# A planned attention and SoLU kernel: loads laid out by partition, and other rules for whom an engine waits

## Chip, cores and metric

One core of one Trainium2 chip runs the whole program. The metric is device time in microseconds, the median of three runs; one more execution is taken by the profiler.

## What is computed

The reference is attention with a local window of 16 positions and block summaries, followed by a two-layer block with a SoLU and a normalisation between its products:

```python
batch, n_heads, seq, head_dim = (4, 8, 768, 64)
block, window = (32, 16)
k_sum = k.reshape(B, H, nb, block, D).max(axis=3)
v_sum = v.reshape(B, H, nb, block, D).mean(axis=3)
scores_l = scale * np.matmul(q, k.transpose(0, 1, 3, 2))
mask_l = np.abs(pos[:, None] - pos[None, :]) < window
scores_s = scale * np.einsum('bhsd,bhnd->bhsn', q, k_sum) + np.log(block)
a = softmax(np.concatenate([np.where(mask_l, scores_l, -1e9), scores_s], axis=-1))
x = np.matmul(a, np.concatenate([v, v_sum], axis=2))    # then (3072, 512)
h = x @ w_in                                            # (3072, 1024)
solu = h * softmax(h)
ln = (solu - mean) / np.sqrt(var + 1e-06) * g_ln
return ln @ w_out                                       # (3072, 512)
```

## The kernel before

The 3072 tokens are 24 tiles of 128 (t). Two tiles make a group of 256 positions (4 windows of 64 positions), three groups (g) a batch (b). Names end in b_g_pp where they belong to an attention unit, which is one group and one half (pp) of the heads: unit 1_0 is group 1, half 0 of a batch. Per unit TensorE forms the scores `s` of 64 positions against a window of 96 keys and 24 block maxima (L498), VectorE takes maxima while adding the mask (L518), ScalarE the exponentials (L526) and their sum z (L531), VectorE its reciprocal (L532), POOL or VectorE the product `e` times 1/z (L245, L246), TensorE transposes (`t`, L552) and multiplies by the values `vt` (`x`, L590). `x` is split into a high and a low part (`xh`, `xl`), and so are the weights, so that each product with w_in (`h`, L616) and w_out (`o`, L681) is three matmuls.

There is one PSUM buffer `h`. Tile t+1 may write it only when VectorE has read tile t twice: the maximum `hm` (L623) and, after ScalarE's exponential `he` (L625), its sum `hz` (L627) and the reciprocal (L628), the product L629. The rest (mean, squares on ScalarE, L636 to L652), the transposes `lt` and `o` follow, `o` three tiles behind.

The weights come as 64-bit numbers in 8 pieces of w_in and 8 of w_out, 512 KB each (`raw`), and are rounded and split by some seven operations a piece (L315 to L334, then L356 to L358 or L238 to L246) on ScalarE, VectorE and POOL, between the attention of the first tiles.

Loads are issued on SyncE's queue. Keys (`kraw`, 400 KB each) are 128 x 800 numbers; queries (`qt`) are 512 KB in pieces of 1 KB, in the first group four loads of 128 KB; the rows of the first batch's values (`st_v`, L388) are three loads of 512 KB in pieces of 2 KB; the windows of values (`vt`, L457) are 768 KB, 96 partitions with four overlapping windows each, in pieces of 2 KB. Into rows 96 to 119 of `vt` ScalarE's queue copies the block means `vsum` (L462), marked as another part of the buffer, so that it need not wait for L457. `LOADS` (L44) is the order of the first loads.

The order on every engine is worked out when the program is built. `Plan.issue` takes each operation with a cost, its data dependences and a due number (the place in the program of the TensorE operation that needs it first), and always starts what can start first; `WAIT` and `FAR` say for whom an engine waits instead, and `RATE` gives a load's duration. Each engine then runs its list strictly in that order, so one operation that waits holds all behind it. Until `FILL` the plan puts short matmuls on zeros (L766, "fillers") where it sees TensorE idle. The rule about waiting is:

```python
            for at, y in ready[e]:
                s = begin(e, at)
                if t < s and s - t < self.WAIT * (t + cost(e, o, t) - s) and y.due + self.FAR < best[1].due:
                    best = (s, y)
```

Of the kernel before, what the change touches and what calls it, by code (L numbers as in the profile page):

```python
# [68 lines left out]
class Plan:  # L69
# [8 lines left out]
    WAIT, FAR = 1.5, 200  # L80
# [49 lines left out]
    def issue(self):  # L130
# [47 lines left out]
        while len(order) < len(self.ops):  # L178
# [32 lines left out]


@with_exitstack
def attn_then_solu(ctx: ExitStack, tc: tile.TileContext, q, k, v, vb, w_in, w_out, g_ln, out):


    nc = tc.nc
    plan = Plan()
    op = plan.op
    pe, act, dve, pool, sp = "pe", "act", "dve", "pool", "sp"  # L220
# [42 lines left out]
    for p0 in (0, QT):  # L263
# [7 lines left out]
            out=m, in_=m, pattern=[[0, 3], [-1, WIN]], compare_op=ALU.is_ge, fill=NEG,  # L271
# [111 lines left out]

    def load_v_rows(b, i):

        rows = v[b, HALO + 2 * P * i:HALO + 2 * P * (i + 1), :].rearrange("(c p) n -> p c n", p=P)
        vst[b, i] = x = plan.buf(sb, [P, 2, 512], F32, "lh" if i < 2 else "ll", 2, f"st_v{b}_{i}")
        op(sp, 0.05, lambda: nc.sync.dma_start(out=x.ap, in_=rows), w=[x], nbytes=P * 4096)  # L388

    def mean_values_first(b):  # L390

# [47 lines left out]
           r=[acc], w=[y])  # L439

    def load_q(b, g, pairs=None, after=()):
        src = q[b, :, :, g * G * QT:(g + 1) * G * QT].rearrange("a p c -> p a c")
        if (b, g) not in qt:
            qt[b, g] = plan.buf(sb, [P, NPAIR, G * QT], F32, "qt", 2, f"qt{b}_{g}")
        x = qt[b, g]
        if pairs is None:
            op(sp, 0.05, lambda: nc.sync.dma_start(out=x.ap, in_=src), w=[x], nbytes=P * 4096,
               after=after)
        else:
# [221 lines left out]
    def second(t):  # L671
# [130 lines left out]
```

## Time and profile before

| | us |
|---|---|
| median of 3 runs | 419.6 (417.32 to 420.45) |
| profiled execution | 419.72 |
| its span, first to last instruction | 417.9 |
| TensorE busy | 396.2 (95%) |
| VectorE busy | 284.1 (68%) |
| ScalarE busy | 243.6 (58%) |
| POOL busy | 124.2 (30%) |
| waits of TensorE's `h` for VectorE's L629 | 6.9 in 7 waits |

PE is TensorE's matmuls and PEld its weight loads, DVE is VectorE, ACT ScalarE, POOL GpSimd, SP SyncE. A busy share is an average over stages with different limits: an engine that is idle elsewhere may be full in the stage that matters. In a timeline row the bracket gives the idle time of the engine just before, and what ended it. The granted clock (PEclk) is a fraction of 2.4 GHz.

### The profile page before, as it was taken

To read this page: it belongs to the slowest core of one execution; us is meant where nothing else is said; L and a number is where in the kernel's file an instruction comes from. 1 tells how busy PE (TensorE), PEld (TensorE's weight loads), DVE (VectorE), ACT (ScalarE), POOL (GpSimd) and SP (SyncE) were. 2 spreads that over 40 slices of the span, in tenths; PEclk is the share of its full clock that TensorE was granted. 3 is DMA by queue.
4 is the path that set the end of the run, shared out by engine and by line. 5 is a ranking of instruction groups with operands and counts; after the bars stand their busy time and mean duration, and the time that the engine had idled before them with its cause. 6 is when DMAs were issued, how large, how long until landed. Compare 5 with 4: busy or idle time off the path is not lost.

```text
span 417.9 us, 9489 instructions
## 1 busy us (share of the span) xinstructions
PE 396.2 (95%) x3667; PEld 299.3 (72%) x3667; DVE 284.1 (68%) x841; ACT 243.6 (58%) x710; POOL 124.2 (30%) x172
## 2 busy tenths in 40 slices
PE   7999598889899999999999999999999999999996
PEld 3437376567678777777877777777777777777876
DVE  4998899996877776736876764564676567453440
ACT  4967889737556745745763673675675566332231
POOL 4676546887851101108102110110110100111010
PEclk9999879999999999999999999999999999999999
DMA  8999996428337412126134220241230000000011
GB/s 268 410 256 263 327 245 164 127 78 197 91 117 200 130 49 80 52 88 153 55 100 124 77 78 27 76 102 40 77 95 29 25 6 23 27 25 2 25 50 52
DMA packets 22929, 46.03 MB, mean 110 GB/s; under 512 B 1860, under 2 KB 8260, under 8 KB 22884
## 3 DMA queue, kind: packets, MB, share of 16 engines
q1 hardware_dynamic: 18096, 36.97, 31.4%
q10 hardware_dynamic: 4788, 8.46, 6.2%
q8 instruction: 29, 0.48, 0.5%
q14 instruction: 16, 0.13, 0.1%
HBM read 36.97 MB, written 6.29 MB: 104 GB/s over the span
## 4 chain that ended last, share of the span: by engine, by line
PE 58%; DMA 16%; DVE 15%; ACT 5%; POOL 3%; issue 1%; SPq 0%; DVEq 0%
PE h L616 26%; PE o L681 22%; DMA kraw<-in_k 4%; DMA vt<-in_v 4%; DMA raw<-in_w_out 4%; DVE hm L623 3%; DVE e L518 3%; DVE he L629 3%; ACT he L625 3%; PE x L590 3%; PE lt L552 3%; DMA st_v<-in_vb 2%; PE t L552 2%; PE s L498 2%; POOL st_v L418 2%; DMA raw<-in_w_in 2%
## 5 line engine op out<-in xcount | busy, mean ns | idle before, releaser
L616 PE MATMUL h<-w,xh 128*128 128x512 f32 x384 | 141.1, 405 | 8.2 <-DVE he L629 6.9
L681 PE MATMUL o<-w,lh 128*128 128x512 f32 (+1 forms) x400 | 142.4, 394 | 0.1
L616 PEld LDWEIGHTS h<-w,xh 128*128 128x128 f32 x384 | 72.4, 189 | 31.8 <-issue 11.0
L681 PEld LDWEIGHTS o<-w,lh 128*128 128x128 f32 x400 | 74.1, 188 | 19.0 <-issue 2.9
L681 PE MATMUL o<-w,ll 128*128 128x512 f32 (+1 forms) x200 | 77.2, 386 | 0.5 <-DVE ll L666 0.5
L616 PE MATMUL h<-w,xl 128*128 128x512 f32 x192 | 75.7, 394 | 0.0
L526 ACT ACTIVATE e<-e,nm 128x120 f32<-128x120 f32 x192 | 73.0, 384 | 1.1 <-DVE nm L518 1.1
L636 POOL TENSOR_SCALAR he<-he,nmu 128x512 f32<-128x512 f32 x27 | 23.8, 883 | 99.5 <-DVE nmu L632 99.3
L625 ACT ACTIVATE he<-h,hm 128x1024 f32<-128x1024 f32 x24 | 26.7, 1114 | 42.9 <-DVE hm L623 42.8
L238 ACT COPY at<-t 120x512 f32<-120x512 f32 x45 | 24.2, 587 | 41.5 <-PE t L552 41.4
L681 PEld LDWEIGHTS o<-w,ll 128*128 128x128 f32 x200 | 37.6, 188 | 8.0 <-DVE ll L666 0.8
L518 DVE CUSTOM_DVE_ANT_0 e<-s,mask 128x120 f32<-128x120 f32 x192 | 40.5, 275 | 2.8 <-PE s L498 2.8
L616 PEld LDWEIGHTS h<-w,xl 128*128 128x128 f32 x192 | 36.3, 189 | 6.8
L623 DVE TENSOR_REDUCE hm<-h 128x1 f32<-128x1024 f32 x24 | 29.3, 1221 | 14.9 <-PE h L616 14.9
L240 POOL COPY kw<-ksum 128x192 f32<-128x192 f32 (+1 forms) x26 | 9.4, 363 | 100.6 <-PE s L498 79.9
L641 ACT ACTIVATE sq<-he 128x1024 bf16<-128x1024 f32 x24 | 25.4, 1057 | 22.6 <-POOL he L636 20.6
L239 DVE CAST lh<-lt 128x512 fp32r<-128x512 f32 x23 | 15.8, 687 | 32.4 <-PE lt L552 27.1
L666 DVE TENSOR_TENSOR ll<-lt,lh 128x512 fp32r<-128x512 f32 x48 | 31.8, 684 | 8.5 <-ACT lh L238 8.1
L418 POOL TENSOR_TENSOR st_v<-st_v 96x512 f32<-96x512 f32 (+3 forms) x42 | 33.9, 816 | 8.8 <-DMA st_v<-in_vb 6.3
L526 ACT ACTIVATION_READ_ACCUMULATOR e<-e,nm 128x1 f32 x192 | 36.3, 189 | 0.0
L590 PEld LDWEIGHTS x<-at,vt 120*64 120x64 f32 (+1 forms) x768 | 25.4, 141 | 10.4 <-issue 5.2
L629 DVE SCALAR_TENSOR_TENSOR he<-h,hz,he 128x1024 f32<-128x1024 f32 x24 | 30.7, 1278 | 0.2
(79 smaller groups left out, 525.3 us busy)
## 6 DMA issues: line engine op xcount, KB each, us to landing
vt<-in_v SPq DMA_DIRECT2D x12, 768.0 KB, 5.8
kraw<-in_k SPq DMA_DIRECT2D x16, 400.0 KB, 7.5
out<-os ACTq DMA_DIRECT2D x23, 256.0 KB, 2.0
qt<-in_q SPq DMA_DIRECT2D x11, 512.0 KB, 4.0
st_v<-in_vb SPq DMA_DIRECT2D x12, 384.0 KB, 3.7
raw<-in_w_in SPq DMA_DIRECT2D x8, 512.0 KB, 7.1
raw<-in_w_out SPq DMA_DIRECT2D x8, 512.0 KB, 12.0
vt<-vsum ACTq DMA_DIRECT2D x11, 192.0 KB
```

What stands on the lines that cost most here:

```text
L238: by = {act: lambda: nc.scalar.copy(out=to(), in_=of()), dve: lambda: nc.vector.tensor_copy(out=to(), in_=of()), pool: lambda: nc.gpsimd.t ...
L418: op(pool, 0.15 + w * 0.0021, lambda w=w, o=o: nc.gpsimd.tensor_tensor(out=o.ap[:n, :w], in0=x.ap[:n, :w], in1=x.ap[:n, w:2 * w], op=ALU.add),
L518: nc.vector.tensor_tensor_reduce(out=e.ap[:, n, :], in0=sc.ap[:, j, (2 * i + up) * KC:(2 * i + up + 1) * KC], in1=mask[:, mi, :], scale=-S ...
L526: nc.scalar.activation(out=e.ap[:, n, :], in_=e.ap[:, n, :], func=AF.Exp, bias=nm.ap[:, n:n + 1], scale=-1.0, accum_out=z.ap[:, n:n + 1])
L590: nc.tensor.matmul(xp.ap[j * D:(j + 1) * D, i, qs], vs.ap[:k, u, cs], at.ap[:k, u % 2, n[j] + u // 2, :], start=not apart, stop=not apart ...
L616: nc.tensor.matmul(o, a.ap[:, c, ts], w.ap[:, i], start=(c == 0 and n == 0), stop=(c == NKC - 1 and n == 2))
L623: op(dve, 1.13, lambda: nc.vector.tensor_reduce(out=nm.ap, in_=h.ap, op=ALU.max, axis=AX.X, negate=True), r=[h], w=[nm])
L625: op(act, 1.09, lambda: nc.scalar.activation(out=e.ap, in_=h.ap, func=AF.Exp, bias=nm.ap, accum_out=z.ap), r=[h, nm], w=[e, z])
L629: op(dve, 1.27, lambda: nc.vector.scalar_tensor_tensor(out=e.ap, in0=h.ap, scalar=z.ap, in1=e.ap, op0=ALU.mult, op1=ALU.mult, accum_out=s1 ...
L641: op(act, 1.13, lambda: nc.scalar.activation(out=sq.ap, in_=e.ap, func=AF.Square, accum_out=ss.ap), r=[e], w=[sq, ss])
L666: op(dve, 0.6, lambda part=part, r=r: nc.vector.tensor_tensor(out=part(lo), in0=tp.ap[:, r], in1=part(hi).bitcast(F32), op=ALU.subtract), ...
L681: nc.tensor.matmul(o.ap[:, cols], a.ap[:, f, :], w.ap[:, i, cols], start=(f == 0 and n == 0), stop=(f == NFC - 1 and n == 2))
```

## The change

Arrays are laid out on the host so that what a partition gets in one load lies in one piece of memory: keys by pairs, queries by group (4 KB a partition; the first group in two loads of 256 KB instead of four), the value rows (4 KB) in an array of their own, and the windows of values over 128 partitions (8 KB each, 1 MB; rows 96 to 127 are zeros). The window load now writes the whole buffer, so the copy of the block means comes after it. In the plan, `RATE` goes from 360 to 400, `WAIT` from 1.5 to 4.0 and `FAR` from 200 to 40: an engine waits for what is due 40 places earlier, not 200, and up to four times as long as the wait saves.

```diff
-LOADS = "kqkqkqkqwwwwwwwwrrrvQV"
+LOADS = "kqkkqkwwwwwwwwrrrvQV"
...
-    RATE = 360.0
+    RATE = 400.0
...
-    WAIT, FAR = 1.5, 200
+    WAIT, FAR = 4.0, 40
...
-        op(sp, 0.05, lambda: nc.sync.dma_start(out=x.ap[:, i], in_=k[b, p]), w=[(x, i)], nbytes=P * SP * 4,
+        op(sp, 0.05, lambda: nc.sync.dma_start(out=x.ap[:, i], in_=k[b, pp, :, i]), w=[(x, i)], nbytes=P * SP * 4,
...
-        rows = v[b, HALO + 2 * P * i:HALO + 2 * P * (i + 1), :].rearrange("(c p) n -> p c n", p=P)
-        op(sp, 0.05, lambda: nc.sync.dma_start(out=x.ap, in_=rows), w=[x], nbytes=P * 4096)
+        op(sp, 0.05, lambda: nc.sync.dma_start(out=x.ap, in_=vr[i]), w=[x], nbytes=P * 4096)
...
-            op(sp, 0.05, lambda: nc.sync.dma_start(out=x.ap[:, pairs], in_=src[:, pairs]),
-               w=[(x, pairs)], nbytes=P * 1024)
+        part = slice(None) if pairs is None else slice(2 * pairs, 2 * pairs + 2)
+        op(sp, 0.05, lambda: nc.sync.dma_start(out=x.ap[:, part], in_=q[b, g, :, part]),
+           w=[x] if pairs is None else [(x, 2 * pairs), (x, 2 * pairs + 1)],
+           nbytes=P * 4096 if pairs is None else P * 2048, after=after)
...
-        op(sp, 0.05, lambda: nc.sync.dma_start(out=x.ap[:WIN], in_=src), w=[(x, 0)], nbytes=WIN * 8192,
+        op(sp, 0.05, lambda: nc.sync.dma_start(out=x.ap, in_=v[b, g]), w=[x], nbytes=P * 8192,
...
+    vw = np.zeros((B, NG, P, G, DM), v.dtype)
+    vw[:, :, :WIN] = vp[:, windows].reshape(B, NG, G, WIN, DM).transpose(0, 1, 3, 2, 4)
```

Line numbers shift by the change: of before L317, L323, L326, L330 are L318, L324, L327, L331 of after, L462 is L457, L518 is L513, L532 is L527, L623 is L618, L625 is L620, L628 is L623, L629 is L624.

The first place is VectorE's list around the statistics of tile 0, before (`raw_141` and `raw_143` are the third and fourth pieces of w_out, `hm_591` the maximum, `z_1_0` the sum of unit 1_0; L629 comes next):

```order
L317 TENSOR_SCALAR raw_141<-raw_141 128x512
L323 TENSOR_SCALAR raw_141<-raw_141 128x512
L326 TENSOR_SCALAR cv_out_562<-raw_141 128x512
L330 SCALAR_TENSOR_TENSOR raw_141<-raw_141 128x512
L317 TENSOR_SCALAR raw_143<-raw_143 128x512
L623 TENSOR_REDUCE hm_591<-h_428 128x1
L326 TENSOR_SCALAR cv_out_562<-raw_143 128x512
L532 RECIPROCAL z_1_0_549<-z_1_0_549 128x8
L518 ISA e_1_1_605,nm_1_1_606<-s_1_1_574,mask 128x120
L330 SCALAR_TENSOR_TENSOR raw_143<-raw_143 128x512
L628 RECIPROCAL hz_603<-hz_603 128x1
L358 SCALAR_TENSOR_TENSOR w_616<-cv_out_562,g_sb,w_616 128x512
```

After, at the same place (`raw_139` is now the third piece of w_out, `hm_572` the maximum):

```order
L324 TENSOR_SCALAR raw_139<-raw_139 128x512
L327 TENSOR_SCALAR cv_out_545<-raw_139 128x512
L331 SCALAR_TENSOR_TENSOR raw_139<-raw_139 128x512
L618 TENSOR_REDUCE hm_572<-h_403 128x1
L527 RECIPROCAL z_1_0_535<-z_1_0_535 128x8
L513 ISA e_1_1_583,nm_1_1_584<-s_1_1_555,mask 128x120
L623 RECIPROCAL hz_579<-hz_579 128x1
L624 SCALAR_TENSOR_TENSOR he_578,s_602<-h_403,hz_579,he_578 128x1024
```

The fourth piece has moved behind the whole chain of tile 0, and nothing of the weights stands between its maximum and its product any more.

The second place is ScalarE's list around the copy of the block means into the windows of group 2, before (`w` are halves of w_in, `raw_137` the first piece of w_out):

```order
L238 CAST xh_0_479<-x_0_1_458 128x512
L462 DMA vt_2_507<-vsum_415 24x4x512
L238 CAST w_509<-cv_in_330 128x512
L315 ACTIVATE raw_137<-raw_137 128x512
L238 COPY kw_2_0_517<-kraw_0_93 128x8x96
```

After (`raw_143` and `raw_145` are the fifth and sixth pieces of w_out, `he_772` is the exponential of tile 1):

```order
L526 ACTIVATE z_1_1_597<-z_1_1_597 128x8
L316 ACTIVATE raw_143<-raw_143 128x512
L457 DMA vt_2_638<-vsum_388 24x4x512
L322 ACTIVATE raw_143<-raw_143 128x512
L316 ACTIVATE raw_145<-raw_145 128x512
L322 ACTIVATE raw_145<-raw_145 128x512
L239 COPY kw_2_1_604<-kraw_1_102 128x8x96
L239 COPY at_1_1_764<-t_1_1_726 120x512 x2
L620 ACTIVATE he_772,hz_773<-h_648,hm_745 128x1024
```

The copy has moved from the end of the attention of group 0 to the middle of the weight conversions of w_out, ahead of the exponential of tile 1.

## Rows read from the trace of the kernel before

**Rows 1.** The page: busy time of the engines, and GB/s in 40 slices.

```profile
PE 396.2 (95%) x3667; PEld 299.3 (72%) x3667; DVE 284.1 (68%) x841; ACT 243.6 (58%) x710; POOL 124.2 (30%) x172
...
GB/s 268 410 256 263 327 245 164 127 78 197 91 117 200 130 49 80 52 88 153 55 100 124 77 78 27 76 102 40 77 95 29 25 6 23 27 25 2 25 50 52
```

**Rows 2.** Busy time by stages cut at `h` starts; columns in the first row.

```profile
core 0: us, PE busy (x) PEld busy (x) DVE busy (x) ACT busy (x) POOL busy (x), PEclk, DMA share, GB/s
...
30.87:42.85 11.98, 11.81 (x137) 8.14 (x136) 9.78 (x26) 8.61 (x20) 6.87 (x6) 1.00 1.04 258
42.85:52.65 9.80, 5.03 (x68) 3.74 (x68) 9.16 (x30) 7.98 (x30) 5.36 (x4) 0.84 1.05 331
52.65:68.36 15.71, 14.02 (x168) 10.90 (x168) 15.36 (x40) 13.93 (x41) 7.99 (x6) 0.88 1.01 245
68.36:84.90 16.54, 13.31 (x135) 10.10 (x135) 15.60 (x36) 13.55 (x37) 12.49 (x16) 1.00 0.41 120
...
97.56:109.41 11.85, 10.66 (x72) 8.25 (x72) 7.86 (x31) 8.47 (x27) 9.24 (x14) 1.00 0.69 186
...
160.00:400.00 240.00, 238.63 (x2191) 187.01 (x2190) 146.92 (x468) 131.59 (x387) 36.46 (x56) 1.00 0.20 59
```

**Rows 3.** Timeline of TensorE: start, duration, work [idle before it <- releaser].

```profile
50.09 1.11 PE L552 MATMUL t<-ident,e 64*120 64x64 f32 x16 [4.77 <-POOL e L246]
...
52.65 0.76 PE L616 MATMUL h<-w,xh 128*128 128x512 f32 x1
...
84.90 0.50 PE L616 MATMUL h<-w,xh 128*128 128x512 f32 x1 [2.63 <-DVE he L629]
```

**Rows 4.** Timeline of VectorE around the statistics of tile 0.

```profile
43.23 0.44 DVE L317 TENSOR_SCALAR raw<-raw 128x512 f32<-128x512 f32 x1 [2.59 <-DMA raw<-in_w_out]
...
45.19 1.40 DVE L317 TENSOR_SCALAR raw<-raw 128x512 f32<-128x512 f32 x1 [0.26 <-DMA raw<-in_w_out]
46.51 1.21 DVE L623 TENSOR_REDUCE hm<-h 128x1 f32<-128x1024 f32 x1
...
47.97 0.19 DVE L532 RECIPROCAL z<-z 128x8 f32<-128x8 f32 x1
...
49.66 0.92 DVE L330 SCALAR_TENSOR_TENSOR raw<-raw 128x512 int32<-128x512 int32 x1
...
51.23 1.27 DVE L629 SCALAR_TENSOR_TENSOR he<-h,hz,he 128x1024 f32<-128x1024 f32 x1
```

**Rows 5.** Timeline of ScalarE at the same place.

```profile
41.54 0.38 ACT L526 ACTIVATE e<-e,nm 128x120 f32<-128x120 f32 x1
...
45.76 0.19 ACT L531 ACTIVATE z<-z 128x8 f32<-128x8 f32 x1
...
47.75 1.11 ACT L625 ACTIVATE he<-h,hm 128x1024 f32<-128x1024 f32 x1 [1.24 <-DVE hm L623]
```

**Rows 6.** Stretches as in rows 2; the last columns are DMA share and GB/s.

```profile
22.00:36.00 14.00, 13.68 (x137) 6.30 (x141) 14.00 (x14) 9.03 (x16) 11.25 (x8) 1.00 1.08 230
36.00:44.00 8.00, 7.83 (x86) 5.79 (x79) 5.41 (x24) 6.36 (x20) 3.00 (x3) 1.00 1.02 290
44.00:50.00 6.00, 1.32 (x12) 0.93 (x10) 5.75 (x23) 4.24 (x14) 3.53 (x3) 0.97 1.03 380
50.00:58.00 8.00, 7.91 (x66) 6.00 (x67) 7.88 (x15) 6.25 (x23) 5.08 (x4) 0.60 1.08 232
...
312.00:313.00 1.00, 1.00 (x6) 0.78 (x6) 0.06 (x1) 0.72 (x3) 0.40 (x1) 1.00 0.13 41
```

**Rows 7.** VectorE's groups from 42.9 to 110 us: count, busy us, mean ns, idle before.

```profile
L330 DVE SCALAR_TENSOR_TENSOR raw<-raw 128x512 int32<-128x512 int32 x8 | 6.8, 848 | 0.0
...
L358 DVE SCALAR_TENSOR_TENSOR w<-cv_out,g_sb,w 128x512 fp32r<-128x512 f32 x8 | 6.2, 793 | 0.0
...
L380 DVE TENSOR_REDUCE ksum<-kraw 128x24 f32<-128x768 f32 x6 | 5.6, 939 | 0.0
...
L245 DVE TENSOR_TENSOR e<-e,z 128x960 f32<-128x960 f32 x3 | 4.3, 1426 | 0.0
```

More of the change, by code (lines that the diff above doesn't have):

```diff
@@ L213, in attn_then_solu @@
 @with_exitstack
-def attn_then_solu(ctx: ExitStack, tc: tile.TileContext, q, k, v, vb, w_in, w_out, g_ln, out):
+def attn_then_solu(ctx: ExitStack, tc: tile.TileContext, q, k, v, vr, vb, w_in, w_out, g_ln, out):
     nc = tc.nc
@@ L441, in load_q @@
     def load_q(b, g, pairs=None, after=()):
-        src = q[b, :, :, g * G * QT:(g + 1) * G * QT].rearrange("a p c -> p a c")
         if (b, g) not in qt:
@@ L445, in load_q @@
         x = qt[b, g]
[L446 to L449, printed above, removed]
-            op(sp, 0.05, lambda: nc.sync.dma_start(out=x.ap[:, pairs], in_=src[:, pairs]),
-               w=[(x, pairs)], nbytes=P * 1024)
+        part = slice(None) if pairs is None else slice(2 * pairs, 2 * pairs + 2)
+        op(sp, 0.05, lambda: nc.sync.dma_start(out=x.ap[:, part], in_=q[b, g, :, part]),
+           w=[x] if pairs is None else [(x, 2 * pairs), (x, 2 * pairs + 1)],
+           nbytes=P * 4096 if pairs is None else P * 2048, after=after)
     def load_v(b, g, after=()):
         vt[b, g] = x = plan.buf(sb, [P, G, DM], F32, "vt", 2, f"vt{b}_{g}")
-        rows = v[b, g * G * QT:g * G * QT + WIN, :]
-        src = bass.AP(rows.tensor, rows.offset, [[DM, WIN], [QT * DM, G], [1, DM]])
-        op(sp, 0.05, lambda: nc.sync.dma_start(out=x.ap[:WIN], in_=src), w=[(x, 0)], nbytes=WIN * 8192,
+        op(sp, 0.05, lambda: nc.sync.dma_start(out=x.ap, in_=v[b, g]), w=[x], nbytes=P * 8192,
            after=after)
@@ L696, in attn_then_solu @@
         "k": [lambda p=p: load_keys(0, p) for p in range(NPAIR)],
-        "q": [lambda p=p: load_q(0, 0, p) for p in range(NPAIR)],
+        "q": [lambda p=p: load_q(0, 0, p) for p in range(NPP)],
         "w": [lambda c=c: load_w_in(*c) for c in w_in_pieces],
@@ L776 @@
     q, k, v = inputs["q"], inputs["k"], inputs["v"]
-    qT = np.ascontiguousarray(q.transpose(0, 1, 3, 2)).reshape(B, NPAIR, P, S)
-    kp = np.zeros((B, NPAIR, P, SP), k.dtype)
-    kp[..., HALO:HALO + S] = k.transpose(0, 1, 3, 2).reshape(B, NPAIR, P, S)
+    qT = q.transpose(0, 1, 3, 2).reshape(B, NPAIR, P, NG, G * QT).transpose(0, 3, 2, 1, 4)
+    kp = np.zeros((B, NPP, 2, P, SP), k.dtype)
+    kp[..., HALO:HALO + S] = k.transpose(0, 1, 3, 2).reshape(B, NPP, 2, P, S)
+    rows = v.transpose(0, 2, 1, 3).reshape(B, S, DM)
     vp = np.zeros((B, SP, DM), v.dtype)
-    vp[:, HALO:HALO + S] = v.transpose(0, 2, 1, 3).reshape(B, S, DM)
+    vp[:, HALO:HALO + S] = rows
+    windows = np.arange(NU)[:, None] * QT + np.arange(WIN)
+    vw = np.zeros((B, NG, P, G, DM), v.dtype)
+    vw[:, :, :WIN] = vp[:, windows].reshape(B, NG, G, WIN, DM).transpose(0, 1, 3, 2, 4)
     arrays = {
-        "q": qT,
-        "k": kp,
-        "v": vp,
+        "q": np.ascontiguousarray(qT),
+        "k": np.ascontiguousarray(kp.transpose(0, 1, 3, 2, 4)),
+        "v": vw,
+        "vr": np.ascontiguousarray(rows[0].reshape(3, 2, P, DM).transpose(0, 2, 1, 3)),
         "vb": np.ascontiguousarray(v).reshape(B, 2, 4 * NB, BLOCK * D),
```

## The prediction

> **What bounds the kernel now.** I read the page's busy times and its DMA slices first [rows 1], then a table of stages cut at the starts of the `h` products [rows 2], then TensorE's timeline at the gaps between them [rows 3], and last the two engines that TensorE waits for there [rows 4, 5] and the DMA by stretch [rows 6].
>
> TensorE is busy for 396.2 of 417.9 us [rows 1]. From 160 to 400 us it idles 1.37 of 240 us [rows 2]: that part is its own work and nothing here shortens it. What can be won lies before 110 us. There each tile's `h` product must wait until VectorE has read the last one out of the only `h` buffer (maximum L623, then L629, both on VectorE, with ScalarE's exponential L625 between). `h` of tile 0 ends at 42.85 and that of tile 1 starts at 52.65, 9.8 us later, and in that stretch TensorE is busy 5.03 us, part of it with fillers [rows 2]. The reader should see three things. First, the transposes `t` of unit 1_0 sat idle for 4.77 us, until 50.09, and run 1.11 us; the granted clock, 0.84 on average in this stage, is 0.88 in the next, so TensorE fell to the lower of its two levels (1.2 GHz) after that gap. A gap of 2.63 us, before 84.90 [rows 3], left the stage 68.36 to 84.90 at 1.00 [rows 2]. Second, VectorE is busy for 9.16 of 9.80, 15.36 of 15.71 and 15.60 of 16.54 us from 42.85 to 84.90 [rows 2]: it is the bound of the early tiles. Third, at 43.23 VectorE had stood 2.59 us for a `w_out` load, and once more 0.26 us at 45.19, with the maximum of tile 0 queued behind these conversions until 46.51 [rows 4].
>
> **The change, part by part.** The profiled execution took 419.72 us, 1.82 us more than its span; the median of the runs shown is 419.6, so the sum is made against 419.72.
>
> Start up to the end of tile 0's `h` (42.85): the same bytes of k, q and w_in come first, and the products wait on the conversions, for VectorE is the full engine there (9.78 of 11.98 us from 30.87 on, [rows 2]) and stays so. Before the score maxima of unit 1_0 the new order gives VectorE five subtractions of weights instead of four and gives POOL two instead of four, while ScalarE starts the first exponentials only behind the first weight piece. I cannot price this from rows. The bounds are a loss or a gain of 2 us (some two operations of 0.8 to 1.4 us on VectorE, as in [rows 7]); I take 0, because one operation comes and others go.
>
> `h` of tile 0 to `h` of tile 1. The new VectorE order puts one piece of w_out, not two and a half, ahead of the maximum, and takes L326, L330 and L358 out from behind it. With h_0 ending at 42.85: maximum 1.2 us, to 44.1. ScalarE's eight exponentials of unit 1_0 run from 41.54 to about 44.7 (0.38 us each), the sum's copy L531 (0.19) to 44.9, then L625 from 44.9 to 46.1 (1.11 and its read-out), hz to 46.4 [rows 5]. VectorE takes z's reciprocal at 45.0, the eight score maxima (1.6 us, what lies between the reciprocal at 47.97 and L330 at 49.66) to 46.7, hz at 46.8, L629 from 46.9 to 48.2 (1.27; all of VectorE's in [rows 4]). Tile 1's `h` starts near 48.35 instead of 52.65: **4.3 us won**. The transposes of unit 1_0 came 2.1 us behind z's reciprocal before (47.97 to 50.09: POOL's product and the start), so they come near 47.1; the fillers ended at 45.3 (50.09 less 4.77), and the gap is about 1.8 us, below the 2.63 us that kept the clock. The restored clock adds nothing to the sum, since VectorE and not TensorE decides the next starts.
>
> Tile 1 to tile 4 (52.65 to 97.56 before). VectorE is full, so I count its work from one L629 to the third next in both orders. The new order has two more L326, one L330, one L358, two scalings L317, one L323 and one cast: 2 x about 0.8 + 0.85 + 0.79 + about 2.8 for the last four = 6.0 us more; and three fewer k maxima L380, two fewer L245 and nine fewer of the small steps behind `sq`: 3 x 0.94 + 2 x 1.43 + about 2.9 = 8.6 us less [rows 7]. That is **2.6 us less ahead of tile 4**. The other bound is none of it, where VectorE waits instead; since a shorter queue waits more often for ScalarE and POOL, I give back **1.0 us** (estimate: the one wait of that kind before, on POOL, was about that long).
>
> Tile 4 to 5 (97.56 to 109.41 before, 11.85 us, [rows 2]): the VectorE work put off returns here, three k maxima among it, but VectorE had 4 us idle in that stretch (7.86 of 11.85), so it fits. TensorE brings three `o` products fewer to that point, 0.7 us of work that it still owes: **0.7 us lost**. From there the order of TensorE is the same to the last tile but for small exchanges: 0.
>
> Loads. From 22 to 58 us the queue is crowded: 230, 290, 380 and 232 GB/s [rows 6], 269 by time. The change cuts the pieces of q, of the value rows and of the windows from 1 and 2 KB to 4 and 8 KB, and adds a third to the bytes of the windows. The end of a window load before shows only 0.13 of the DMA engines still busy (312 to 313, [rows 6]): the 96-partition load is unevenly shared, so I expect at least 300 GB/s. The bounds are 230 (no better than the worst stretch) and 400 (the best whole slice has 410, [rows 1]). This costs or wins nothing by itself as long as two pieces land in time. The third piece of w_out is wanted at about 42; 12.3 MB stand before its landing (k 1.6, q 0.5, w_in 4.2, rows 1.6, two windows 2.1, the next q 0.5, three pieces of w_out 1.6, a copy 0.2), 7.1 of them moved by 20.9 us (two slices of 10.45 us at 268 and 410 GB/s, [rows 1]), so 5.2 remain: 33.9 at 400, 43.5 at 230. The second is below, as a rival.
>
> The Trainium skill, DMA: Bandwidth & Descriptors, section Specifications, names 512 bytes as the smallest transfer for line rate. By it pieces of 1 KB were full already, and the Trainium skill, on that page under Why a DMA increments its semaphore by 16, gives 16 engines to 96 partitions as to 128. The idle engines at 312 us show that sixteen engines need not end together; whether longer pieces are faster no row shows. By the Trainium skill the rate stays, and the time becomes that of rival (b).
>
> Sum: 0 + 4.3 + 2.6 - 1.0 - 0.7 = 5.2 us; 419.7 - 5.2 = **414.5 us**.
>
> **The rivals.** (a) The start is worse. In the new order VectorE must wait for z of unit 0_0 behind twelve exponentials, and POOL no longer helps with two subtractions; the lower bound of that stage, 2 us, comes true: 416.5. For it: VectorE is the bound there. Against: fewer POOL operations beside VectorE's.
>
> (b) The loads stay at 269 GB/s. The copy of the mean values into the windows (L462, now L457) must now wait for the window's own load, since both write its last rows. For unit group 2 it stands on ScalarE at about 55 us (hz of tile 0 at 46.4, then some 8.5 us of exponentials, copies and weight conversions). 17.0 MB stand before that landing (the 12.3 above, five more weight pieces 2.6, two q 1.0, a window 1.0, rounded), so 9.9 after 20.9 us: at 269 it lands at 57.7, and ScalarE, with L625 of tile 1 behind it, stands for 2.7 us: 417.2.
>
> (c) Slower: the same wait at 230 GB/s. The window lands at 63.9, ScalarE stands 8.9 us, VectorE's queue waits for the weights behind it and `h` of tile 2 comes as much later: 419.7 - 5.2 + 8.9 = 423.4. It decides from 250 GB/s down, where the wait exceeds 5.2 us; above 290 it is gone. For it: that rate stands in two stretches of [rows 6]. Against: both hold the short pieces that go.
>
> (d) More is won: nothing is given back to waits (1.0) and the start wins its 2 us: 419.7 - 8.2 = 411.5. For it: every load lands earlier. Against: VectorE is the bound, not DMA.
>
> **How the numbers follow.** Forecast 0.42, (a) 0.17, (b) 0.17, (c) 0.12, (d) 0.12. One per cent is 4.2 us, about what a measurement of this kernel can tell from no change; the line is 415.4. The forecast's own spread of 2 us leaves two thirds of it below that line; with (d) and a small part of (a) that makes 0.45 faster. (a), (b), the rest of the forecast and the milder part of (c) make 0.47 the same. More than half of (c), 0.08, lies beyond one per cent, since at that rate the nine later copies, each behind eight exponentials in the new order, may wait as well. The range goes from 410.5, under (d), to 420.5, which leaves out most of (c).
>
> **What would show it.** Right: `h` of tile 1 starts by 49 us, the gap before the transposes of 1_0 is under 2.7 us and the clock stays at 1.00; `h` of tile 5 starts 5 to 6 us earlier; 160 to 400 us is unchanged. Wrong: VectorE still stands for w_out before the maximum of tile 0; or ScalarE stands before a window copy; or the lead at tile 1 is gone by tile 5, which would say that something other than VectorE's queue sets the early tiles.

## The result and the profile after

The changed kernel takes **422.1 us** (median of 15 runs, 419.6 to 424.2); the kernel before took 419.4 beside it (417.2 to 422.55). The ratio is **1.0075, interval 1.0052 to 1.0098**: slower, by less than one per cent. The forecast was 414.5, with 410.5 to 420.5 as its range, and both missed. The profiled execution took 420.28 us (span 418.6), so it is 1.8 us below its own median; a comparison of the two traces can explain only a part of the 2.6 us.

The page after, which answers to [rows 1]:

```profile
PE 397.4 (95%) x3646; PEld 298.4 (71%) x3646; DVE 278.4 (67%) x836; ACT 246.8 (59%) x714; POOL 125.9 (30%) x173
...
GB/s 267 411 411 343 140 311 145 91 47 237 121 136 228 130 98 56 71 100 147 59 121 121 77 102 27 77 110 56 78 107 39 27 7 22 26 27 0 27 50 52
```

The loads run at 411 GB/s in the third slice too, where they had 256, and at 343 in the fourth, which had 263. TensorE's busy time has not shrunk.

The stages, cut at the same events as [rows 2]: end of `h` of tile 0 (45.10), then the starts of `h` of tiles 1 to 6.

```profile
core 0: us, PE busy (x) PEld busy (x) DVE busy (x) ACT busy (x) POOL busy (x), PEclk, DMA share, GB/s
...
45.10:49.99 4.89, 3.30 (x61) 2.51 (x62) 4.67 (x23) 4.83 (x21) 3.36 (x3) 1.00 0.54 168
49.99:65.63 15.64, 11.80 (x161) 9.18 (x161) 15.22 (x37) 12.57 (x40) 8.74 (x6) 0.98 0.89 321
65.63:81.94 16.31, 13.58 (x133) 10.66 (x133) 16.27 (x37) 14.19 (x42) 9.97 (x9) 0.91 0.21 63
...
95.08:106.69 11.61, 11.07 (x85) 8.38 (x84) 9.26 (x37) 7.28 (x26) 9.35 (x13) 1.00 0.73 216
106.69:126.44 19.75, 19.62 (x217) 15.08 (x218) 14.22 (x59) 12.88 (x42) 13.67 (x22) 1.00 0.46 135
...
160.00:400.00 240.00, 237.25 (x2183) 185.34 (x2181) 145.33 (x463) 134.46 (x390) 34.78 (x54) 1.00 0.20 64
```

The first row is the gain that the forecast named: 4.89 us from `h` of tile 0 to `h` of tile 1, where there were 9.8. The next two are the disappointment: 15.64 and 16.31 us, against 15.71 and 16.54, with VectorE full in both. `h` of tile 5 starts at 106.69, still 2.7 us earlier than before; then the stage to tile 6 takes 19.75 us with TensorE full (before: 17.81, from 109.41 to 127.22). That is less of a loss than it looks: the stage now holds 33 `o` products where it held 27, 1.4 us of work that stood in other stages before.

TensorE's timeline at the gaps, as in [rows 3]:

```profile
48.79 0.33 PE L547 MATMUL t<-ident,e 64*120 64x64 f32 x3 [1.29 <-POOL e L247]
...
65.63 0.80 PE L611 MATMUL h<-w,xh 128*128 128x512 f32 x1 [3.39 <-DVE he L624]
...
81.94 0.59 PE L611 MATMUL h<-w,xh 128*128 128x512 f32 x1 [2.73 <-DVE he L624]
...
196.21 0.69 PE L547 MATMUL t<-ident,e 64*120 64x64 f32 x16 [1.06 <-DVE ss L638]
```

and the clock from 10 to 20 us and around the gaps of 3.39 and 2.73 us:

```profile
core 0: us, PE busy (x), PEclk, DMA share, GB/s
10.00:20.00 10.00, 10.00 (x66) 0.83 1.03 412
...
62.00:65.00 3.00, 0.24 (x3) 1.00 0.97 390
65.00:69.00 4.00, 3.37 (x9) 0.57 0.12 51
82.00:86.00 4.00, 4.00 (x11) 0.57 0.25 79
86.00:90.00 4.00, 4.00 (x20) 1.00 0.25 83
```

The gap of 4.77 us is down to 1.29 and the clock holds there. But the gaps before `h` of tiles 2 and 3 are now 3.39 and 2.73 us, and TensorE comes out of each at its lower level (1.2 GHz). The `h` of tile 2 runs 7.12 us and that of tile 3 7.35, where they ran 5.75 and 5.77 at the upper level. A gap of 2.63 us had cost nothing before [rows 3]; behind it the trace of before has a clock of 1.00:

```profile
84.90:90.67 5.77, 5.77 (x25) 1.00 0.07 18
```

The clock also falls to 0.83 from 10 to 20 us, where it was 1.00.

VectorE's two weight steps from `h` of tile 1 to `h` of tile 3 (count, busy us, mean ns, idle before), to be held against [rows 7]:

```profile
L331 DVE SCALAR_TENSOR_TENSOR raw<-raw 128x512 int32<-128x512 int32 x7 | 7.9, 1169 | 0.0
L359 DVE SCALAR_TENSOR_TENSOR w<-cv_out,g_sb,w 128x512 fp32r<-128x512 f32 x6 | 7.1, 1203 | 0.0
```

They were 848 and 793 ns. Two operations of the same line and shape show why. At 49.76, with GpSimd idle, L359 takes 0.75 us; at 69.08, beside GpSimd's product, it takes 2.04:

```profile
49.76 0.75 DVE L359 SCALAR_TENSOR_TENSOR w<-cv_out,g_sb,w 128x512 fp32r<-128x512 f32 x1
```

```profile
69.08 2.04 DVE L359 SCALAR_TENSOR_TENSOR w<-cv_out,g_sb,w 128x512 fp32r<-128x512 f32 x1
```

```profile
68.78 1.79 POOL L247 TENSOR_TENSOR e<-e,z 128x960 f32<-128x960 f32 x1 [0.83 <-DVE z L527]
```

In what follows **excess** is the sum, over VectorE's operations from the start of `h` of tile 1 to that of tile 3, of the time of each above the shortest of its line and shape in the same trace. It is 6.97 us before and 8.95 after. The Trainium skill, GPSIMD Engine Reference, section 1 (Specifications), says that GpSimd shares its way to SBUF with VectorE and contends with VectorE's instructions that run in a 2-port mode or have two SBUF inputs; the rows above agree, with 0.75 against 2.04 us. A step with one input can run longer too: L327 took 0.42 us at 44.33, with GpSimd idle, and 1.55 at 56.50, beside GpSimd's additions (L335). It is a place where the forecast should have looked: its [rows 7] gave only a mean.

### The profile page after: what moved, and what is told of

It is laid out like the page before. It is cut to its first block, busy times and chain, and to the rows that moved or that the text cites. A ratio compares the mean times of both kernels' runs of the same rounds, so it can differ in the third digit from the quotient of the medians.

```text
span 418.6 us, 9444 instructions
## 1 busy us (share of the span) xinstructions
PE 397.4 (95%) x3646; PEld 298.4 (71%) x3646; DVE 278.4 (67%) x836; ACT 246.8 (59%) x714; POOL 125.9 (30%) x173
## 4 chain that ended last, share of the span: by engine, by line
PE 59%; DVE 22%; ACT 5%; DMA 5%; issue 4%; POOL 3%; ACTq 1%; SPq 0%; DVEq 0%; POOLq 0%
PE h L611 26%; PE o L676 20%; DVE e L513 5%; DVE hm L618 4%; DVE he L624 4%; ACT he L620 3%; PE vs_ps L761 3%; PE t L547 2%; PE lt L547 2%; PE x L585 2%; DVE raw L331 2%; DMA vt<-in_v 2%; PE s L493 2%; DMA st_v<-in_vb 2%; DVE ksum L381 1%
## 5 line engine op out<-in xcount | busy, mean ns | idle before, releaser
L611 PE MATMUL h<-w,xh 128*128 128x512 f32 x384 | 143.2, 410 | 10.8 <-DVE he L624 8.5
L611 PEld LDWEIGHTS h<-w,xh 128*128 128x128 f32 x384 | 73.6, 192 | 35.8 <-issue 8.9
L611 PE MATMUL h<-w,xl 128*128 128x512 f32 x192 | 76.9, 401 | 0.5 <-DVE xl L591 0.5
L620 ACT ACTIVATE he<-h,hm 128x1024 f32<-128x1024 f32 x24 | 26.7, 1114 | 39.0 <-DVE hm L618 39.0
L513 DVE CUSTOM_DVE_ANT_0 e<-s,mask 128x120 f32<-128x120 f32 x192 | 40.5, 275 | 2.6 <-PE s L493 2.6
L618 DVE TENSOR_REDUCE hm<-h 128x1 f32<-128x1024 f32 x24 | 29.3, 1219 | 12.6 <-PE h L611 12.6
L241 POOL COPY kw<-ksum 128x192 f32<-128x192 f32 (+1 forms) x26 | 8.5, 332 | 89.9 <-PE s L493 79.3
L681 ACT ACTIVATE os<-o,y 128x512 f32<-128x512 f32 (+1 forms) x20 | 13.3, 666 | 31.4 <-PE o L676 31.4
```

Of the source, the lines that this page charges most:

```text
L513: nc.vector.tensor_tensor_reduce(out=e.ap[:, n, :], in0=sc.ap[:, j, (2 * i + up) * KC:(2 * i + up + 1) * KC], in1=mask[:, mi, :], scale=-S ...
L611: nc.tensor.matmul(o, a.ap[:, c, ts], w.ap[:, i], start=(c == 0 and n == 0), stop=(c == NKC - 1 and n == 2))
L618: op(dve, 1.13, lambda: nc.vector.tensor_reduce(out=nm.ap, in_=h.ap, op=ALU.max, axis=AX.X, negate=True), r=[h], w=[nm])
L620: op(act, 1.09, lambda: nc.scalar.activation(out=e.ap, in_=h.ap, func=AF.Exp, bias=nm.ap, accum_out=z.ap), r=[h, nm], w=[e, z])
```

## The experiments

Each of the experiments ran in 5 to 12 timed runs beside the kernel before; they ran on three chips, so the ratios compare better than the medians. "Clock" is the mean granted clock over the runs (before: 0.987).

| run | ratio to before | interval | median us | clock | excess us |
|---|---|---|---|---|---|
| changed kernel | 1.0075 | 1.0052 to 1.0098 | 422.1 | 0.984 | 8.95 |
| e1 96 rows, same order | 1.0075 | 1.0042 to 1.0107 | 421.5 | 0.983 | 8.33 |
| e2 old WAIT, FAR | 1.0045 | 1.0008 to 1.0082 | 419.9 | 0.983 | 7.77 |
| e3 only WAIT, FAR | 1.0026 | 0.9992 to 1.0060 | 419.2 | 0.990 | 11.12 |
| e4 96 rows, planned | 1.0070 | 1.0034 to 1.0106 | 421.6 | 0.985 | 7.36 |
| e5 layout alone | 0.9978 | 0.9944 to 1.0011 | 418.1 | 0.987 | 5.72 |
| e6 RATE 360 | 0.9953 | 0.9924 to 0.9981 | 416.8 | 0.998 | 4.86 |
| e7 old first loads | 1.0055 | 1.0028 to 1.0082 | 420.6 | 0.984 | 6.25 |
| e8 layout, WAIT, FAR | 1.0011 | 0.9978 to 1.0043 | 419.5 | 0.984 | 7.54 |
| x9 more fillers early | 1.0051 | 1.0029 to 1.0073 | 421.2 | 0.987 | 9.57 |
| x10 no GpSimd adds | 0.9990 | 0.9964 to 1.0017 | 418.3 | 0.985 | 6.08 |
| x11 RATE 400, port told | 1.0195 | 1.0171 to 1.0219 | 427.0 | 0.975 | 8.11 |
| x12 RATE 360, port told | 0.9893 | 0.9871 to 0.9915 | 414.7 | 0.997 | 4.21 |
| y1 RATE 380 | 1.0031 | 1.0005 to 1.0056 | 419.9 | 0.989 | 7.56 |
| y2 RATE 340 | 0.9910 | 0.9876 to 0.9944 | 414.5 | 0.996 | 4.54 |
| y3 RATE 420 | 1.0033 | 1.0007 to 1.0058 | 419.0 | 0.989 | 4.80 |
| y4 RATE 360, old WAIT, FAR | 1.0063 | 1.0030 to 1.0097 | 420.6 | 0.986 | 8.34 |
| z1 RATE 360, fewer fillers | 1.0000 | 0.9968 to 1.0033 | 419.4 | 0.986 | 2.11 |
| z2 RATE 340, port told | 1.0082 | 1.0049 to 1.0115 | 422.5 | 0.985 | 3.50 |

### Is it ScalarE's wait for the window? (e1, e2, e3, e4)

The trace after shows rival (b)'s wait, in the late part:

```profile
193.40 0.82 ACTq L457 DMA_DIRECT2D vt<-vsum  x1
194.27 0.21 ACT L526 ACTIVATE z<-z 128x8 f32<-128x8 f32 x1 [3.02 <-DMA vt<-in_v]
```

So the first theory (W) was that the window wait costs the time; the rival (O) was the new order alone.

```diff
# e1: in load_v, the plan unchanged
-  nc.sync.dma_start(out=x.ap, in_=v[b, g]), w=[x], nbytes=P * 8192
+  nc.sync.dma_start(out=x.ap[:WIN], in_=v[b, g, :WIN]), w=[x], nbytes=P * 8192
# e4: as e1, with the plan told
+  ..., w=[(x, 0)], nbytes=WIN * 8192
# e2, on the changed kernel
-  WAIT, FAR = 4.0, 40
+  WAIT, FAR = 1.5, 200
# e3, on the kernel before
-  WAIT, FAR = 1.5, 200
+  WAIT, FAR = 4.0, 40
```

> The changed kernel with its window loads cut to the 96 rows that hold values (768 KB instead of 1 MB, still 8 KB a partition). The order of every engine is that of the changed kernel; all that goes is the copy's wait for the load, and a quarter of the bytes. Theory W (the changed kernel loses by ScalarE standing at L457 for the window load: 0.90 us at 55.9, 2.2 at 131.1 and 3.02 at 194.3 in its profile): these three waits go, the 1.06 us gap of TensorE at 196.2 with them, and the time falls by 1.5 to 3.5 us from 422.1, to 418.5 to 420.5, a ratio to before of 0.998 to 1.003. Theory O (it loses by the new order alone, two-operand work of VectorE and GpSimd meeting, and the gaps before h): 421.3 to 423, ratio 1.005 to 1.009.

> The changed kernel with window loads of 96 rows, and the plan told so (the copy is free of the load, 768 KB each), so that the order is made anew. Theory W: like the first of these or a little better, 416 to 420, since the copies go back to the place before their loads. Theory O: as slow as the changed kernel, 421 to 424.

> The changed kernel with WAIT, FAR of before (1.5, 200); layouts, order of first loads and RATE 400 stay new. Theory W: the copy still waits for its own load, so it stays slow, 421 to 424. Theory O: the loss goes and the faster loads are left, 415 to 418.5.

> The kernel before with only WAIT, FAR 4.0, 40; all loads, LOADS and RATE as before. Theory W: no copy waits for its window, so the new order alone is the same or faster, 416 to 419.5. Theory O: slower, 421 to 424.

W fell: e1 and e4 are as slow as the changed kernel. The wait was also shorter than the row says. Its 3.02 us count the issue of two transfers as idle; the copy itself could have gone out at 192.2, when the issue before it ended, and went at 193.40, so it stood for 1.2 us. In the same way the 0.90 us at 55.9, which theory W counts, is nearly all the copy's own issue (0.80 us). In e1 the copy hardly waits (it goes out at 192.33), but GpSimd, which had stood 1.63 us for its next rows of values in the changed kernel, stood 2.95:

```profile
192.54 1.29 POOL L418 TENSOR_TENSOR st_v<-st_v 96x512 f32<-96x512 f32 x1 [2.95 <-DMA st_v<-in_vb]
```

and TensorE had a gap of 3.17 us before `h` of tile 11 (1.06 and 0.36 us at that place in the changed kernel). So a late load does cost something near 190 us, whichever engine stands for it, and e1 doesn't price the window's own part. e2 gives neither theory its figure; e3, at 419.2, lies within that of W and below that of O. Each half of the change alone lies 0.3 to 0.5% above before, with intervals that reach close to or over 1.

### Layout, RATE, first loads (e5 to e8)

```diff
# e5, on the kernel before: k, q, value rows and windows (96 rows) from the new arrays, plan untouched
-  in_=k[b, p]
+  in_=k[b, pp, :, i]
...
-  src = q[b, :, :, g * G * QT:(g + 1) * G * QT].rearrange("a p c -> p a c")
+  src = q[b, g]
# e6, on the changed kernel
-  RATE = 400.0
+  RATE = 360.0
# e7, on the changed kernel, with q in four loads
-  LOADS = "kqkkqkwwwwwwwwrrrvQV"
+  LOADS = "kqkqkqkqwwwwwwwwrrrvQV"
# e8: e5 with WAIT, FAR = 4.0, 40
```

> The kernel before with nothing changed but where the arrays lie: keys, queries, value rows and windows in one piece per partition, windows still 96 rows, first queries still in four loads, RATE, WAIT, FAR and LOADS of before, so every engine has the order of before. Theory P (the plan's new numbers and load order cost the time, the layout helps): VectorE's wait of 2.59 us for w_out before 43.23 goes, h of tile 1 starts 2 to 3 us earlier, and the time falls by 1 to 4 us, ratio 0.990 to 0.998. Theory N (VectorE's and GpSimd's work bounds the early tiles, loads are covered): ratio 0.998 to 1.002. Theory B (faster landing itself hurts, since it bunches work): ratio 1.003 to 1.008, as in the run with the old WAIT and FAR.

> The changed kernel with RATE 360 again, all else new. Theory P with RATE as its number: back to 417 to 420, ratio 0.997 to 1.003. Theories N and B, and P with another number: as the changed kernel, ratio 1.005 to 1.009.

> The changed kernel with the order of the first loads of before (k and q in turn, q in four loads of 128 KB), all else new. Theory P with LOADS as its number: h of tile 0 ends 1 to 3 us earlier than in the changed kernel (45.10) and the ratio to before is 0.997 to 1.003. Otherwise as the changed kernel, 1.005 to 1.009.

> The layout alone (e5) with WAIT, FAR 4.0, 40. Theory P: WAIT and FAR cost 0.3% as they did on the old layout (ratio 1.0026 there): 0.3% above e5. Theory O2 (the two changes help each other, since the longer waits fit the faster loads): at or below e5, and h of tile 1 starts by 49 us.

**RATE alone is the largest step of all: 1.0075 with 400, 0.9953 with 360**, intervals far apart, 5.3 us in medians. With RATE 360 the change does part of what was forecast: 0.5% faster than before (416.8), where 1.2% was forecast. The stages of e6 that answer to 49.99:65.63 and 65.63:81.94 above:

```profile
51.44:63.56 12.12, 10.41 (x130) 8.26 (x130) 12.07 (x34) 11.88 (x36) 5.70 (x5) 1.00 0.92 323
63.56:78.21 14.65, 12.32 (x131) 9.14 (x131) 13.35 (x20) 11.69 (x26) 10.26 (x9) 1.00 0.25 80
```

The two stages take 5.2 us less, 12.12 and 14.65 us instead of 15.64 and 16.31, at a clock of 1.00; 1.5 of these had been lost before them (`h` of tile 1 starts at 51.44, not 49.99). VectorE is busy for 6.1 us less in them, of which the excess makes 4.1. L359 is back at its short form (739 ns against 1203 above), though L331 is not (1058 against 1169), and some score maxima and weight steps have moved out of the stretch:

```profile
L331 DVE SCALAR_TENSOR_TENSOR raw<-raw 128x512 int32<-128x512 int32 x7 | 7.3, 1058 | 0.0
...
L359 DVE SCALAR_TENSOR_TENSOR w<-cv_out,g_sb,w 128x512 fp32r<-128x512 f32 x5 | 3.7, 739 | 0.0
```

The old first loads (e7) change nothing that can be told from the changed kernel. The layout alone (e5), in the order of before, lies at 0.9978, between the figures of theories P and N, and can't be told from no change; `h` of tile 1 starts at 54.15 in its trace, not earlier than before as P had it. e8 lies 0.3% above e5, as P had it, with overlapping intervals; O2's early start of `h` of tile 1 did not come (54.72). e5 shows something else: most of the faster loading doesn't come from the longer pieces. The stretch 22 to 36 us (last columns DMA share and GB/s), e5 first and the changed kernel after it:

```profile
22.00:36.00 14.00, 1.00 1.03 256
```

```profile
22.00:36.00 14.00, 1.00 1.02 411
```

e5 has pieces of 4 and 8 KB and windows of 96 partitions: 256 GB/s, little above the 230 of before [rows 6], with the engines as busy. From 26 to 32 us e1, which differs from the changed kernel in the 96 rows alone, has 226 GB/s and the changed kernel 408; e4 (96 rows) has 223 and e6 (128 rows) 407. So the 128 partitions bring the rate. It brings no time here: e1 and the changed kernel have the same ratio, 1.0075.

### What RATE does (y1 to y4)

```diff
# y1, y2, y3, on the changed kernel
-  RATE = 400.0
+  RATE = 380.0   (340.0, 420.0)
# y4, on the changed kernel
-  RATE = 400.0
+  RATE = 360.0
-  WAIT, FAR = 4.0, 40
+  WAIT, FAR = 1.5, 200
```

> The changed kernel with RATE 380. Theory R (RATE itself decides: the list begins differently from some value between 360 and 400 on; with 380 the start on TensorE is as with 360, the first transposes after 14 fillers, not 31): as with 360, ratio 0.992 to 0.999. Theory L (luck of the list: any small change of a number gives another order, good or bad): anywhere from 0.99 to 1.02, and no trend over the four values.

> The changed kernel with RATE 340. Theory R: as with 360, ratio 0.992 to 0.999. Theory L: anywhere from 0.99 to 1.02.

> The changed kernel with RATE 420. Theory R: it starts as with 400 and is as slow, ratio 1.004 to 1.011. Theory L: anywhere from 0.99 to 1.02.

> The changed kernel with RATE 360 and WAIT, FAR 1.5, 200: what WAIT and FAR are worth where RATE is not raised. If they gain there (as the forecast had it: VectorE free for the statistics of tile 0), this is slower than with RATE 360 alone (0.9953): 0.998 to 1.006, and h of tile 1 starts 3 us later than its 51.44. If they cost 0.3% as on the old loads, 0.990 to 0.994.

From 340 to 400 the ratio climbs: 0.9910, 0.9953, 1.0031, 1.0075; 420 gives 1.0033. Theory R, a step at the changed start, is out, since 380 starts like 360 and is 0.8% slower than it. y4 says what the other part of the change is worth: with RATE 360, WAIT and FAR bring the ratio from 1.0063 to 0.9953. With RATE 400 the same numbers bring it from 1.0045 (e2) to 1.0075, intervals overlapping. The parts don't add. In y4's trace `h` of tile 1 starts at 55.01, 3.6 us later than in e6, as that expectation had it; but 2.8 of these stand before the end of `h` of tile 0 (47.84 against 45.09), and only 0.8 between that and tile 1. (The profiled execution of y4, 424.0, is its slowest.)

### The clock (x9, z1)

```diff
# x9, on the changed kernel: 4, 2 and 5 more fillers between the first groups of scores
+        EXTRA = [0, 4, 2, 5]
         for o in order:
             if o.engine == "pe":
+                for _ in range(EXTRA.pop(0) if EXTRA else 0):
+                    self.keep_up(1e9, done)
# z1, on the changed kernel with RATE 360: 12 fillers fewer there
-                while at + self.SYNC < min(o.start, self.FILL):
+                while at + self.SYNC < min(o.start, self.FILL) and not 6.5 < o.start < 12.5:
```

> The changed kernel with 11 more fillers on TensorE between the first four groups of score products (4, 2 and 5), so that the gaps of 1.39 and 0.39 us before 8.72 and 9.75 are nearly filled; the rest of every engine's order stays. Theory K (TensorE's clock: in 70 executions of the kernel before a mean clock lower by 0.004, one stretch of 3.4 us at the lower level, goes with 0.8 us more; the changed kernel has 0.984 on average, the one with RATE 360 0.998): the fall at 10.5 us goes, and the median falls by 0.8 us or more, to 419.5 to 421.3. Theory S (VectorE's operations run longer beside GpSimd's, and the order with RATE 400 puts more of them together): what happens at 10 us is not on the path, 421.3 to 422.5.

> The changed kernel with RATE 360 and without the 12 fillers of TensorE between the first groups of score products (1, 2 and 9 of them); every other instruction of every engine stands as with RATE 360. It is the reverse of the run with more fillers. Theory K: the granted clock falls near 10 us, the mean clock drops from 0.998 to 0.990 or below, and the time rises by 0.8 us for each 0.004, to 418 to 420. Theory S: VectorE's overlaps with GpSimd are as with RATE 360 (4.86 us between h of tile 1 and of tile 3), and the time stays, 416 to 417.6.

z1 is the cleaner of the two: no instruction but fillers of zeros has gone, and **the time rises from 0.9953 to 1.0000**, with intervals that just overlap. Its own runs point the same way: the four at a clock of 0.991 or 0.992 took 417.0 to 417.3 us, the eight at 0.988 or lower 418.2 to 422.5. Its clock in the first 50 us, by tens:

```profile
0.00:10.00 10.00, 6.80 (x59) 0.98 0.81 271
10.00:20.00 10.00, 7.62 (x56) 0.67 1.03 415
20.00:30.00 10.00, 9.84 (x53) 1.00 1.02 412
30.00:40.00 10.00, 9.77 (x102) 0.85 1.00 391
40.00:50.00 10.00, 10.00 (x94) 0.81 0.06 16
```

e6 has 1.00 in all five. In z1's profiled execution `h` of tile 0 starts at 41.41, in e6's at 38.05, and `h` of the last tile is still 5.0 us later (384.36 and 379.34); these two executions (421.1 and 416.0) lie further apart than the medians, 2.6 us. In x9 the fall at 10 us is gone (1.00 from 10 to 20, 0.83 in the changed kernel), and the median fell by 0.9 us, with overlapping intervals; its clock falls later, after gaps of 3.92 and 3.14 us before `h` of tiles 2 and 3. In 139 executions of the kernel before, those at 0.9815 or lower (26) average 420.2 us and those at 0.9915 or higher (35) 417.5.

### VectorE beside GpSimd (x10, x11, x12, z2)

```diff
# x10, on the changed kernel, in rounded()
-  op(pool, 1.46, lambda: nc.gpsimd.tensor_tensor(out=to(), in0=to(), in1=low(), op=ALU.add),
+  op(pool, 1.46, lambda: key < 2 * NKC and nc.gpsimd.tensor_tensor(out=to(), in0=to(), in1=low(), op=ALU.add),
# x11, on the changed kernel; x12 the same with RATE 360, z2 with RATE 340
-  r=[(x, 1)], w=[(x, 0)])
+  r=[(x, 1)], w=[(x, 0)], port=True)
...
-  r=[(st, f % 2), (hl, 0), g_b], w=[(hl, 1)])
+  r=[(st, f % 2), (hl, 0), g_b], w=[(hl, 1)], port=True)
```

> The changed kernel in its own order, with GpSimd's eight additions at L335 for w_out left out (the low parts of w_out are not added). Theory S: VectorE's operations between the starts of h of tile 1 and tile 3 take 8.95 us more than the shortest of their form in the changed kernel; without these additions that falls below 5, h of tile 3 starts 3 to 5 us earlier (77 to 79), and the time is 417 to 419.5. Theory K: the gaps stay, 420.5 to 422.5.

> The changed kernel with port=True on VectorE's L331 and on L359, so that the plan counts that they run longer while GpSimd works, as it does for the other steps of the weights; the order is made anew. Theory S: less lies together, 417 to 420.5. Theory K: no change that follows from it, 420.5 to 423.

> The changed kernel with RATE 360 (416.8, ratio 0.9953) and the same two port=True. Theory S: at or below that, 413.5 to 416.5, if the plan's picture of the port is good enough to help. Theory K: what decides is whether the gaps stay short in the new order, 415.5 to 420.

> The changed kernel with RATE 340 and port=True on L331 and L359, which with RATE 360 gave 0.9893 and with RATE 400 1.0195. If a lower RATE and the port are worth something each by themselves: 0.985 to 0.990. If it is the luck of each order: between 0.985 and 1.005, and its time follows the mean clock and VectorE's long operations of its own profile.

Without GpSimd's eight additions, in the same order, the time falls from 1.0075 to 0.9990, as theory S had it, while the clock stays where it was (0.984 and 0.985). L331 runs 876 ns there and L359 1026, instead of 1169 and 1203. The excess falls to 6.08 only, and `h` of tile 3 starts at 80.69 and not by 79: right in kind, half the size. Leaving the additions out also frees ScalarE's next step on these weights from waiting for GpSimd, so the whole 3.6 us can't be put down to the overlap.

Telling the plan of the port is no rule. With RATE 360 it gives the lowest ratio of all (**x12: 414.7 us, ratio 0.9893, interval 0.9871 to 0.9915**, ahead of both kernels; y2 with RATE 340 alone, 0.9910, can't be told from it). It makes the kernel slower with 400 (1.0195) and 340 (1.0082), and there neither theory's figure holds. z2 has a small excess, 3.50 us, and is slow; its gaps before `h` of tile 1 (2.52 us) and the transposes at 91.7 (2.18) take the clock down.

## Why the prediction was wrong

The sum was 5.2 us to win. Read between the same events of the two traces, up to the start of `h` of the last tile, it came out like this:

| | forecast | profiled pair |
|---|---|---|
| start, to the end of `h` of tile 0 | 0 | -2.2 |
| `h` of tile 0 to tile 1 | 4.3 | 4.8 |
| tile 1 to tile 4 | 2.6 - 1.0 | -0.2 |
| tile 4 to the last | -0.7 | -3.0 |
| sum | 5.2 | -0.5 |

The term that the forecast built on came true. Three steps failed: the start taken at nothing, VectorE's work from tile 1 to 4 priced at means, and "after that 0".

**Start, "I take 0".** Mis-sized: `h` of tile 0 ended 2.2 us later (45.10 against 42.93 in the same reading of both traces), rival (a)'s bound. The wait that (a) named, VectorE's for z, is not in the trace, so (a) had the size only. VectorE stood 1.5 us longer for the first keys (6.0 against 4.5), 1.3 us for a transpose and, longest of the new waits, for a weight cast: ScalarE stood 2.60 us for the mean of the value rows with the cast queued behind it, and VectorE then 2.18 us for that cast. In the kernel before (first row), ScalarE stood there as long, but no cast stood right behind, and VectorE had no wait of that kind. How much of the 2.2 us each of them makes is not shown.

```profile
29.72 0.58 ACT L404 COPY vsum<-vs_ps 24x512 f32<-24x512 f32 x1 [2.76 <-PE vs_ps L400]
```

```profile
29.43 0.58 ACT L404 COPY vsum<-vs_ps 24x512 f32<-24x512 f32 x1 [2.60 <-PE vs_ps L400]
```

```profile
30.69 0.69 DVE L246 TENSOR_TENSOR w<-cv_in,w 128x512 fp32r<-128x512 f32 x1 [2.18 <-ACT w L239]
```

**Tile 0 to tile 1, 4.3 us won.** Right, in mechanism and size: 4.89 us instead of 9.72 between the same two events, the wait for w_out gone, the gap 1.29 us and the clock at 1.00 there.

**Tile 1 to tile 4, 2.6 us less work, 1.0 given back.** Here the sum failed. The forecast counted VectorE's operations and priced them at the means of before. From L629 of tile 0 to that of tile 3 the counts came out as forecast, but the operations took 49.93 us against 50.31: 0.4 us less, not 2.6. One more L330 and one more L358 were priced at 1.6 us; these two lines together took 6.9 us more (seven in 8.18 and eight in 9.51 us, where it had been six in 5.18 and seven in 5.62), since the new order puts them beside GpSimd's work. From `h` of tile 1 to `h` of tile 4 it took 45.09 us (49.99 to 95.08); before it was 44.91. Nothing was won where 1.6 was forecast.

**"The restored clock adds nothing."** Right at that one gap, and left out everywhere else: the clock fell at 10 us and after the gaps of 3.39 and 2.73 us instead, and `h` of tiles 2 and 3 ran 1.4 and 1.6 us longer. Behind the first of these gaps that was hidden, since VectorE was busy for 16.27 of 16.31 us; behind the second TensorE was busy throughout (13.14 us to `h` of tile 4, 12.66 before). (The stage that the forecast cites for the gap of 2.63 us ends with that gap; the row behind it, shown above, has 1.00 too.) The forecast looked at one gap and not at where the next would open; z1 puts the fillers that hold the clock near 10 us at about half a per cent.

**Tile 4 to 5, 0.7 lost; after that 0.** The three `o` products were owed as stated (36 before `h` of tile 5, 39 in the kernel before), and the 19.75 us to tile 6 hold them and three more. What failed is the 0 after that. From tile 4 to the last, TensorE was busy 2.1 us longer (283.97 against 281.85) and idle 0.9 us longer. Of the 2.1, 1.1 were also owed at tile 4: the sixteen products that make the block means of the next batch, which stood ahead of it in the kernel before:

```profile
92.81 1.07 PE L433 MATMUL vs_ps<-vacc,ident 96*24 96x64 f32 x16
```

The largest single loss is the one from tile 10 to tile 11, 1.7 us (1.4 us ahead at its start, 0.3 behind at the end), with the same number of products in a slightly different order: TensorE stood 1.06 us for the transposes, which waited for ScalarE's z behind the window copy, and 0.36 us for `h`. So a wait of the kind of rivals (b) and (c) did come, 1.2 us long, at one of the later copies that (c) had named and not where it was priced. The stretch from 160 to 400 us is not unchanged: TensorE idles 2.75 us there, before 1.37. The other 1.0 us of longer work is not explained.

**Loads.** The forecast of at least 300 GB/s was right (411), with some luck in its reason. The 96 partitions were what held the rate down, as e1, e4 and e5 show, but not because engines stood idle: with 96 partitions the DMA share is 1.03 (e5), with 128 it is 1.02. In the traces' DMA records from 22 to 36 us a packet of 8 KB took 0.57 to 0.60 us in e1, e4 and e5 and 0.32 in the changed kernel and e6; why, no run here shows. And the row on which the forecast rests, 0.13 from 312 to 313 us, is not the end of the window load: every packet that starts in it belongs to ScalarE's queue, which carries the copy of the block means. The Trainium skill, DMA: Bandwidth & Descriptors, section Specifications, asks only for 512 bytes: e5 agrees that longer pieces add little. By the Trainium skill, on the same page under Why a DMA increments its semaphore by 16, 96 partitions get all 16 engines like 128; the rate at equal pieces, 226 against 408 GB/s, says that this is not the whole story. The rates of rivals (b) and (c), 269 and 230 GB/s, did not arise early, and e1 says that they would not have decided: it has the low rate and the same time.

**What was not priced at all is RATE.** The forecast read the new order at three places and summed these, and that order is the one of RATE 400; that the same layouts and the same WAIT and FAR with another RATE give another order of every engine, worth 5 us, is in none of its terms nor its rivals. With RATE 360 the measured time lies 2.3 us above the forecast, inside its range. Against y4 WAIT and FAR gain 1.1% there; that they gain it for the reason that was given, the earlier statistics of tile 0, is not shown, since the stage from the end of `h` of tile 0 to tile 1 is only 0.8 us shorter.

What stays open: why the list gets worse with RATE. The ratio climbs from 340 to 400, but 420 and the runs with the port break the row, so a large part may be which order happens to come out. The rivals there, the clock and VectorE beside GpSimd, each cost time, as z1 shows and x10 suggests, but the 5 us of RATE are not divided between them: z1 has the smallest excess of all, 2.11 us, and no gain. And of the 2.6 us between the medians the profiled pair shows 0.56; the lower clock of the changed kernel's runs (0.984 against 0.987) goes with about 0.5 us more in the kernel before, and the rest is not located.

## What to carry to other kernels

When a number of a scheduler is changed, every list is new: price the change by what it does to overlaps and gaps over the whole run, and try the neighbouring values of that number before judging the rest of the change by it. Count a busy engine's work with the time of an operation alone and beside its neighbour, not with a mean, and look at the order for which of the two it will be. A filler that keeps the clock belongs to the order as much as the work: twelve of them were worth about half a per cent.

## What the runs showed of the hardware

- Window loads over 96 partitions held the queue at 223 to 226 GB/s from 26 to 32 us with pieces of 8 KB; over 128 partitions, a quarter of it zeros, it moved 407 to 408. The DMA share was 1.02 to 1.04 in all of these.
- The same two-input step of VectorE (L359) took 0.75 us alone and 2.04 beside GpSimd's product; a one-input step (L327) 0.42 alone and 1.55 beside GpSimd's additions.
- TensorE kept its clock after a gap of 2.63 us (before) and lost it after one of 2.73 (after); between the same groups of scores it kept it after 1.21 us (before) and lost it after 1.39 (after), but kept it after 1.46 in x12. The gap alone doesn't tell.
